# Bringing row 0 of each tile to all partitions: one DMA three units ahead instead of a matmul and a copy

## The chip, the cores and the metric

The kernel runs on one core of a Trainium2 chip. The metric is the device time of one execution in microseconds (us), median of several runs. Nanoseconds are marked ns. The engines are PE (matrix multiply), PEld (its weight loads), DVE (vector), ACT (scalar, activations), POOL (GpSimd) and SP (here it only issues DMAs).

## The reference

```python
def _attn_ref(x):                          # x: (8, 3008, 256) float32
    X = np.fft.fft(x, axis=1)
    X = np.fft.fft(X, axis=2)
    return X.real.astype(np.float32)

def _moe_ref(x, w_gate, w_val, w_out):     # x: (24064, 256), d_ff = 1536
    g = x @ w_gate
    silu = g * (1.0 / (1.0 + np.exp(-g)))
    val = x @ w_val
    return (silu * val @ w_out).astype(np.float32)
```

A two-dimensional Fourier transform mixes the tokens, then a gated feed-forward block follows. The output is float32 of shape (24064, 256).

## The kernel before

The kernel folds the transform's symmetries. It works on 24 tiles of up to 512 columns (a column stands for two output tokens, "plus" and "minus"). `Pt` and `Qt` hold the two halves of a tile's transform, with the feature index d on partitions. A tile has 12 units, one for each 128 of the 1536 hidden features. In each unit PE makes five matmuls of 512 columns (two gate, one value, and in the next unit's time one more of each) and eight output matmuls of 256 columns for the tile before.

For tiles from the fourth on (`split`), the value path also needs row d=0 of `Qt`, times a weight per hidden feature. That row lies in partition 0, and DVE and ACT need it in all 128 partitions. The kernel gets it there with a matmul whose stationary operand `sel` has ones in row 0 and zeros elsewhere, and an ACT copy from PSUM to the tile `bc`:

```python
psG = tile_pool(name="psG", bufs=3, space=PSUM)   # g: gate and broadcast
psV = tile_pool(name="psV", bufs=3, space=PSUM)   # v: value
psO = tile_pool(name="psO", bufs=2, space=PSUM)   # o: output
bcp = tile_pool(name="bc", bufs=2)
# ... (cut)
SEEDED = (3, 5, 7, 9, 11)
def seed(u):                     # v starts from bc * w0, written by ACT
    seeds[u] = psV.tile([P, T], F32, name="v")
    nc.scalar.activation(seeds[u][:, :w], bc[t][:, :w], AF.Copy, scale=w0[:, f:f + 1])

def part_a(u):                                        # ... (cut)
    g = psG.tile([P, T], F32, name="g")
    mm(g, Wp, 0, Pt, True, False)                                    # L743
    mm(g, Wq, 0, Qt, False, True)
    # ... v from the seed, or a new one
    mm(v, Wp, 1, Pt, not ahead, False)
    nc.scalar.activation(sg[:, :w], g[:, :w], AF.Silu)               # L756
    if ahead:
        nc.scalar.copy(es[:, :w], v[:, :w])                          # L759
    else:
        nc.vector.scalar_tensor_tensor(es[:, :w], bc[t][:, :w], w0[:, f:f + 1], v[:, :w],
                                       op0=Alu.mult, op1=Alu.add)    # L761

def part_b(u):                   # one unit later; ... (cut)
    nc.tensor.matmul(g, Wm, Qt, ...)                                 # L779
    nc.tensor.matmul(v, (Wm if seeded(u) else Wq), Qt, ...)          # L782
    # DVE: vm = 2 es - v (L789); ACT: second Silu of g (L791); DVE: hp = sp * v (L797)

for i, u in enumerate(units):
    t, f = u
    if f == 0 and split(u):
        ps = psG.tile([P, T], F32, name="g")
        nc.tensor.matmul(ps[:, :w], sel, pq_tiles(t)[1][:, :w], start=True, stop=True)   # L919
        bc.pop(t - 2, None)
        bc[t] = bcp.tile([P, T], BF16, name="bc")
        nc.scalar.copy(bc[t][:, :w], ps[:, :w])                                          # L922
    # ... (cut)
    run_loads(3)                 # up to three input loads on SP's queue
    part_a(u)
    if owork: owork.run(4)       # output matmuls of the tile before; every 24th step ends a
                                 # pair: ACT copies it, SP stores it
    # ... seed of the next unit, part_b of the unit before, owork.run(4), folds
    if i in job_at: transform(*job_at[i])   # writes Pt or Qt of a later tile
```

All DMAs of the main loop go through SP's queue, in program order. The kernel orders its instructions by hand; semaphores hold back an instruction until what it reads has been written.

## Time and profile before

| | before |
|---|---|
| time, median of 3 runs | 644.68 us |
| PE busy, of a span of 643.8 us | 632.8 us |
| ACT busy | 532.6 us |
| DVE busy | 522.0 us |
| DMA queue of SP, share of 16 engines | 29.5% |
| broadcast matmuls / copies | 21 / 21 |

The page's busy times and the chain of work that ended last (shares of the span by engine, then by line):

```profile
PE 632.8 (98%) x4179; PEld 405.0 (63%) x4179; DVE 522.0 (81%) x945; ACT 532.6 (83%) x975; POOL 452.3 (70%) x419
...
PE 95%; DVE 2%; POOL 1%; ACT 1%; issue 1%; DVEq 0%; ACTq 0%; POOLq 0%
```

PE bounds this kernel. Now the timeline of PE around the broadcast of one tile. The columns are the start, the modelled duration, engine, line, operation, operands and count:

```profile
308.32 0.60 PE L692 MATMUL o<-Wo,hm 128*128 128x256 bf16 x4
308.76 0.38 PE L919 MATMUL g<-Qt,sel 128*128 128x512 bf16 x1
309.18 0.38 PE L743 MATMUL g<-Pt,Wp 128*128 128x512 bf16 x1
309.39 0.38 PE L743 MATMUL g<-Qt,Wq 128*128 128x512 bf16 x1
```

A matmul's end is modelled by the profile: its duration (0.38 us) is longer than the distance between starts (0.21 us), so durations overlap and a "busy" PE need not be streaming. The starts are what to read. From 309.18 to 309.39 is 0.21 us, the pace of a 512-column stream; the Trainium skill (TensorE: Matmul & The Clock Gate, "Wait — 56ns, not 53.3ns?") measured 215.7 ns for it, and this trace agrees. From the broadcast to the next matmul it is 0.42 us, twice that, although PE counts as busy. ACT at the same time:

```profile
308.46 0.67 ACT L791 ACTIVATE sv<-g 128x512 f32<-128x512 f32 x1
309.18 0.59 ACT L922 CAST bc<-g 128x512 bf16<-128x512 f32 x1
```

The gate matmul starts just after ACT's second Silu has let go of a g buffer (308.46 + 0.67 = 309.13). The whole tile, by the windows view (length; busy time and count of PE, PEld, DVE, ACT, POOL; granted clock; DMA share; GB/s):

```profile
308.76:332.73 23.97, 23.93 (x159) 15.34 (x157) 19.79 (x32) 21.53 (x40) 18.84 (x16) 1.00 0.20 58
```

### The profile page before, as it was taken

The page shows a single profiled execution, that of the slowest core. Times are in us where ns is not written, and L with a number is a line of the kernel's source. Part 1 is how long each engine was busy: PE and PEld are TensorE (multiplying, and loading weights), DVE is VectorE, ACT ScalarE, POOL GpSimd, SP SyncE. Part 2 cuts the span into 40 slices and gives each one's busy share as a digit, 9 for nine tenths or more (in the row PEclk, how much of TensorE's full clock was granted, in tenths as well). Part 3 has the DMA queues.
Part 4 walks back from the last instruction along what each step waited for, and adds up shares of the span by engine and source line. Part 5 has one row for each costly group of instructions (what it writes and reads, how often), then busy time and mean ns, then how long its engine had stood idle before and what let it go on. Part 6 is the DMA issues. An engine that isn't in the chain of part 4 may idle for free.

```text
span 643.8 us, 12739 instructions
## 1 busy us (share of the span) xinstructions
PE 632.8 (98%) x4179; PEld 405.0 (63%) x4179; DVE 522.0 (81%) x945; ACT 532.6 (83%) x975; POOL 452.3 (70%) x419
## 2 busy tenths in 40 slices
PE   8999999999999999999999999999999999999997
PEld 5446666666666666666666666666666666666676
DVE  8788667888888888888888888888888888788872
ACT  7586666888888889888888888888898888988983
POOL 8796854798776898896876777877777434444441
PEclk8999999999999999999999999999999999999999
DMA  9746446344314313435135112125111111111112
GB/s 216 134 71 131 117 116 162 97 131 110 100 50 116 99 37 115 127 98 112 50 97 118 49 35 67 52 76 135 50 44 41 43 41 40 43 50 34 50 50 74
DMA packets 46685, 54.35 MB, mean 84 GB/s; under 512 B 6515, under 2 KB 33691, under 8 KB 46619
## 3 DMA queue, kind: packets, MB, share of 16 engines
q1 hardware_dynamic: 43434, 51.19, 29.5%
q0 software_dynamic: 3184, 2.36, 2.8%
q8 instruction: 32, 0.52, 0.4%
q14 instruction: 35, 0.28, 0.2%
HBM read 29.39 MB, written 24.65 MB: 84 GB/s over the span
## 4 chain that ended last, share of the span: by engine, by line
PE 95%; DVE 2%; POOL 1%; ACT 1%; issue 1%; DVEq 0%; ACTq 0%; POOLq 0%
PE o L692 38%; PE g L743 19%; PE v L743 11%; PE g L779 9%; PE v L782 8%; PE g L587 2%; PE o L587 2%; PE v L799 1%; PE v L438 1%; PE g L438 1%; PE g L919 1%; DVE hp L770 1%; PE g L564 1%; PE o L447 0%; PE o L564 0%
## 5 line engine op out<-in xcount | busy, mean ns | idle before, releaser
L794 POOL TENSOR_TENSOR hm<-sv 128x1024 bf16<-128x1024 f32 (+2 forms) x126 | 234.1, 1858 | 154.1 <-ACT sv L791 133.9
L789 DVE SCALAR_TENSOR_TENSOR sv<-es,v 128x512 f32<-128x512 f32 (+2 forms) x252 | 170.8, 678 | 73.5 <-PE v L782 69.8
L756 ACT ACTIVATE sp<-g 128x512 f32<-128x512 f32 (+2 forms) x252 | 149.3, 593 | 48.3 <-PE g L743 46.5
L692 PE MATMUL o<-Wo,hp 128*128 128x256 bf16 (+2 forms) x1140 | 169.7, 273 | 0.0
L692 PE MATMUL o<-Wo,hm 128*128 128x256 bf16 (+2 forms) x1140 | 169.6, 273 | 0.0
L797 DVE TENSOR_TENSOR hp<-sp,v 128x512 bf16<-128x512 f32 (+2 forms) x252 | 168.9, 670 | 0.0
L791 ACT ACTIVATE sv<-g 128x512 f32<-128x512 f32 (+2 forms) x252 | 162.8, 646 | 6.9 <-PE g L779 6.9
L692 PEld LDWEIGHTS <-hm 128*128 128x128 bf16 (+2 forms) x1140 | 111.9, 98 | 72.3 <-issue 5.3
L692 PEld LDWEIGHTS <-hp 128*128 128x128 bf16 (+2 forms) x1140 | 112.1, 99 | 69.4
L761 DVE SCALAR_TENSOR_TENSOR es<-bc,w,v 128x512 f32<-128x512 bf16 (+2 forms) x147 | 107.5, 731 | 4.2 <-PE v L743 4.2
L743 PE MATMUL g<-Pt,Wp 128*128 128x512 bf16 (+2 forms) x288 | 107.9, 375 | 0.8
L743 PE MATMUL g<-Qt,Wq 128*128 128x512 bf16 (+2 forms) x288 | 107.9, 375 | 0.5 <-DVE Qt L600 0.5
L743 PE MATMUL v<-Pt,Wp 128*128 128x512 bf16 (+2 forms) x288 | 107.8, 374 | 0.1
L779 PE MATMUL g<-Qt,Wm 128*128 128x512 bf16 (+2 forms) x288 | 107.9, 375 | 0.0
L743 PEld LDWEIGHTS <-Wp 128*128 128x128 bf16 x576 | 56.3, 98 | 40.0 <-issue 2.5
L732 ACT ACTIVATE v<-bc,w 128x512 f32<-128x512 bf16 (+2 forms) x105 | 73.2, 697 | 0.5 <-DVE hp L797 0.5
L698 ACT COPY ev<-o 128x512 f32<-128x512 f32 x90 | 53.5, 595 | 8.4 <-PE o L692 5.8
L759 ACT COPY es<-v 128x512 f32<-128x512 f32 (+2 forms) x105 | 60.3, 574 | 0.0
L782 PE MATMUL v<-Qt,Wq 128*128 128x512 bf16 (+2 forms) x147 | 55.1, 375 | 0.0
L743 PEld LDWEIGHTS <-Wq 128*128 128x128 bf16 x324 | 31.6, 98 | 15.7 <-issue 6.6
L157 POOL TENSOR_TENSOR SDf<-XA 128x1020 f32<-128x1020 f32 x14 | 33.0, 2355 | 11.3 <-DMA St<-Fc 6.6
L782 PE MATMUL v<-Qt,Wm 128*128 128x512 bf16 (+2 forms) x105 | 39.4, 375 | 0.0
(175 smaller groups left out, 629.6 us busy)
## 6 DMA issues: line engine op xcount, KB each, us to landing
out_dram<-ev SPq DMA_DIRECT2D x96, 128.0 KB
XA<-in_x_dram SPq DMA_DIRECT2D x32, 256.0 KB
XA<-in_x_dram SPq DMA_DIRECT2D x112, 64.0 KB
XC<-in_x_dram SPq DMA_DIRECT2D x32, 120.0 KB
XC<-in_x_dram SPq DMA_DIRECT2D x105, 32.0 KB
St<-Fc SPq DMA_DIRECT2D x14, 128.5 KB
out_dram<-ev SPq DMA_DIRECT2D x12, 120.0 KB
out_dram<-ev SPq DMA_DIRECT2D x10, 112.0 KB
```

Source lines behind the costliest of these rows:

```text
L692: nc.tensor.matmul(ps[:n, j, :], hts[minus][:, f, c:c + n], Wo[:, f, :], start=(f == 0), stop=(f == nF - 1))
L732: nc.scalar.activation(seeds[u][:, :w], bc[t][:, :w], AF.Copy, scale=w0[:, f:f + 1])
L743: nc.tensor.matmul(ps[:, :w], Wt[:, gv, fs], src[:, :w], start=start, stop=stop, skip_group_check=True)
L756: nc.scalar.activation(sg[:, :w], g[:, :w], AF.Silu)
L759: nc.scalar.copy(es[:, :w], v[:, :w])
L761: nc.vector.scalar_tensor_tensor(es[:, :w], bc[t][:, :w], w0[:, f:f + 1], v[:, :w], op0=Alu.mult, op1=Alu.add)
L779: nc.tensor.matmul(g[:, :w], Wm[:, 0, fs], Qt[:, :w], start=False, stop=True, skip_group_check=True)
L782: nc.tensor.matmul(v[:, :wp], (Wm if seeded(u) else Wq)[:, 1, fs], Qt[:, :wp], start=False, stop=True, skip_group_check=True)
L789: nc.vector.scalar_tensor_tensor(vm[:, w - 1::-1], es[:, :w], 2.0, v[:, :w], op0=Alu.mult, op1=Alu.subtract)
L791: nc.scalar.activation(sm[:, w - 1::-1], g[:, :w], AF.Silu)
L794: nc.gpsimd.tensor_tensor(hts[t][1][:, f - n + 1:f + 1, :w], sv[:, 0:n, :w, 1], sv[:, 0:n, :w, 0], op=Alu.mult)
L797: nc.vector.tensor_tensor(hts[t][0][:, f, :wp], sp[:, :wp], v[:, :wp], op=Alu.mult)
```

## The change

It should take the broadcast off PE and ACT: a DMA, which uses neither, copies row 0 of the next tile's `Qt` to 128 partitions, issued three units before that tile. The fourth tile keeps the matmul, because its row is written only at unit 10 of the tile before.

```diff
-        if f == 0 and split(u):
+        if f == 0 and split(u) and t not in bc:
             ps = psG.tile([P, T], F32, name="g")
             w = width(t) + (B if t == nT - 1 else 0)
             nc.tensor.matmul(ps[:, :w], sel, pq_tiles(t)[1][:, :w], start=True, stop=True)
-            bc.pop(t - 2, None)
             bc[t] = bcp.tile([P, T], BF16, name="bc")
             nc.scalar.copy(bc[t][:, :w], ps[:, :w])
+        if f == 9 and split(u) and t + 1 < nT:
+            w = width(t + 1) + (B if t + 1 == nT - 1 else 0)
+            bc[t + 1] = bcp.tile([P, T], BF16, name="bc")
+            nc.sync.dma_start(out=bc[t + 1][:, :w], in_=pq_tiles(t + 1)[1][0:1, :w].unsqueeze(1).to_broadcast([1, P, w]))
```

## The prediction

> **What bounds the kernel.** The tensor engine. The chain of work that ended last is 95% PE; the page has PE busy for 632.8 of 643.8 us at full clock. The start times in the PE timeline show it closer: from 105 us on one matmul follows the other at the streaming pace (512 columns every 0.216 us), and a unit of a tile takes 1.95 us. ACT (83%) and DVE (81%) keep up; ACT is the closer (21.5 of 24.0 us in a tile without transform work, by the windows view).
>
> **What the change removes.** 20 of 21 broadcast matmuls (line 919) and of 21 ACT copies (line 922, 0.586 us each, 11.7 us of ACT). The matmul alone would be worth 0.216 us, but in the timeline the broadcast starts at 308.76 and the next matmul at 309.18. I read: the broadcast takes one of three g buffers in PSUM, so the gate matmul behind it needs the buffer that ACT's second Silu of two units before (308.46 to 309.13) still reads. Over tiles 5 to 24 the distance to the next matmul is 0.41 to 0.42 us (once 0.37): 8.25 us in sum, half matmul, half buffer wait. All of it is PE time on the critical path; without the broadcast the gate matmul finds a buffer long free.
>
> **What it adds.** 20 DMAs of 128 KB (128 rows of 1 KB, all read from one partition) on SP's queue. By the order of instructions, DVE waits for their landing at a tile's first es, where it waited for ACT. The nearest thing in the trace, the fold spread (128.5 KB, SBUF to SBUF), lands 2.3 to 2.8 us after its issue. The new one reads a single partition: the Trainium skill (SBUF — State Buffer, Door 1: the DMA port swizzle) gives 27.2 GB/s a port, so I estimate 4.8 us for 131 KB, about 7 us to landing if one port limits it; no run here shows that yet. Three units of program order are 5.9 us, too little for that, but SP runs ahead of it: before, it waits from 300.0 to 305.2 for the output copy that comes just after the new DMA, with the next tile at 308.8. So the DMA should go out some 9 us ahead of its tile and land 2 us or more in time; less where input loads are queued.
>
> **What stays.** The wait of 0.13 us per tile for the seed at unit 7, where ACT is late. The rest of ACT's gain hides under PE.
>
> **Time.** 644.68 - 8.25 = 636.4 us, 1.3% less; range 635.4 to 638.6. Faster by over 2%: 0.02; within 2%: 0.93; slower by over 2%: 0.05.
>
> **What the profile would show.** Line 919 once; a tile without transform 23.55 us instead of 23.97; ACT busy 521 us; es at line 761 waiting for PE's v as before, not for a DMA; no new idle time on PE.
>
> **What would make it wrong.** The DMA landing later than its tile's first es: then es, the value buffer's release and PE stall by the difference, up to 20 times. Input loads, or DVE's Q row, ahead of the DMA in SP's queue would do the same. Every eighth DMA waits for an earlier one's landing, so a slow one also holds back stores and loads, but those have slack.

## The result, and the profile after

The changed kernel takes 638.08 us (637.58 to 638.66, 4 runs), the kernel before 644.7 us (4 runs). The ratio is 0.9899, with a 95% interval of 0.9881 to 0.9916. All ratios here are the mean time of one kernel's fast runs over that of the other's of the same rounds, so not quite the ratio of the medians. The output is correct. This is 6.6 us or 1.0% less; 636.4 us were forecast, and the range (635.4 to 638.6) held it, near its upper end. The forecast gain of 8.25 us would be a ratio of 0.9872, outside the interval, so something is missing.

The same parts of the page after; the last line is the group of es on DVE (busy, mean ns of one, idle time before it and what ended it):

```profile
PE 624.6 (98%) x4159; PEld 402.1 (63%) x4159; DVE 518.7 (82%) x945; ACT 520.8 (82%) x955; POOL 452.8 (71%) x419
...
PE 90%; DMA 6%; DVE 2%; SPq 1%; ACT 1%; issue 0%; DVEq 0%; ACTq 0%
...
L761 DVE SCALAR_TENSOR_TENSOR es<-bc,w,v 128x512 f32<-128x512 bf16 (+2 forms) x147 | 107.2, 729 | 3.4 <-DMA bc<-Qt 3.2
```

PE has 20 matmuls and 8.2 us of busy time less, ACT 11.8 us. But DMA now stands in the chain with 6%: the new DMA is 2% of it, and the rest are input loads, mostly at the kernel's start, which the chain reaches by way of SP's queue. And es, which in the kernel before waited only for PE's v (4.2 us), waits 3.2 us for the new DMA. The share of SP's DMA queue rises from 29.5% to 39.3%. PE at the start of the same tile, and that tile in the windows view:

```profile
306.33 0.60 PE L692 MATMUL o<-Wo,hm 128*128 128x256 bf16 x4
306.76 0.38 PE L743 MATMUL g<-Pt,Wp 128*128 128x512 bf16 x1
306.98 0.38 PE L743 MATMUL g<-Qt,Wq 128*128 128x512 bf16 x1
```

```profile
306.76:330.32 23.56, 23.56 (x158) 15.27 (x156) 19.64 (x32) 20.96 (x39) 18.50 (x16) 1.00 0.34 64
```

The gate matmul follows the output matmuls at their pace, and the tile is 0.41 us shorter, as predicted. So most tiles gave what was expected. Where are the other 1.6 us? The waits view has only two waits of es for the DMA (total us, times, longest):

```profile
DVE es L761 <- DMA bc<-Qt: 3.2, 2, 2.0
```

They belong to the 5th and the 10th tile. The 5th in full: first what SP issued, then DVE, then PE. In brackets stands the idle time before an instruction and what ended it.

```profile
119.48 0.84 SPq L704 DMA_DIRECT2D out_dram<-ev  x2
120.37 3.72 SPq L142 DMA_DIRECT2D XC<-in_x_dram  x4
124.14 0.64 SPq L144 DMA_DIRECT2D XC<-in_x_dram  x1
124.82 0.47 SPq L140 DMA_DIRECT2D XC<-in_x_dram  x1
125.39 0.58 SPq L925 DMA_DIRECT2D bc<-Qt  x1
```

```profile
132.10 0.75 DVE L761 SCALAR_TENSOR_TENSOR es<-bc,w,v 128x512 f32<-128x512 bf16 x1 [1.96 <-DMA bc<-Qt]
```

```profile
132.10 0.38 PE L779 MATMUL g<-Qt,Wm 128*128 128x512 bf16 x1
132.90 0.38 PE L782 MATMUL v<-Qt,Wq 128*128 128x512 bf16 x1 [0.42 <-DVE es L761]
133.12 0.49 PE L692 MATMUL o<-Wo,hp 128*128 128x256 bf16 x3
134.03 0.28 PE L692 MATMUL o<-Wo,hp 128*128 128x256 bf16 x1 [0.43 <-DVE hp L797]
```

SP spent 4.8 us issuing six input loads, then issued the broadcast at 125.39, only 3.7 us before the tile's first gate matmul at 129.09. It landed 6.6 us later (from the trace's semaphore updates). es started about 2 us late, and PE lost about 0.6 us at L782 (0.80 between starts instead of 0.22) and 0.6 at the next hp. Compare a quiet tile, the one shown above that starts at 306.76:

```profile
298.00 0.52 SPq L925 DMA_DIRECT2D bc<-Qt  x1
303.19 1.18 SPq L704 DMA_DIRECT2D out_dram<-ev  x3
```

Here the DMA goes out 8.8 us ahead of the tile: SP has nothing left to issue before it, and after it stands waiting for the next output copy until 303.19. It landed at 304.4, over 3 us before it was needed. Of the 20 DMAs, 12 landed more than 2 us before their tile's first es started, six 0.1 to 2 us before it, and two were late.

### The profile page after: what moved, and what is told of

Same layout as the page of the kernel before. It is cut to its first block, busy times and chain, and to the rows that moved or that the text cites. A ratio compares the mean times of both kernels' runs of the same rounds, so it can differ in the third digit from the quotient of the medians.

```text
span 635.8 us, 12736 instructions
## 1 busy us (share of the span) xinstructions
PE 624.6 (98%) x4159; PEld 402.1 (63%) x4159; DVE 518.7 (82%) x945; ACT 520.8 (82%) x955; POOL 452.8 (71%) x419
## 3 DMA queue, kind: packets, MB, share of 16 engines
q1 hardware_dynamic: 46314, 53.77, 39.3%
## 4 chain that ended last, share of the span: by engine, by line
PE 90%; DMA 6%; DVE 2%; SPq 1%; ACT 1%; issue 0%; DVEq 0%; ACTq 0%
PE o L692 38%; PE g L743 18%; PE v L743 10%; PE g L779 9%; PE v L782 8%; DMA XC<-in_x_dram 3%; PE g L587 2%; DMA bc<-Qt 2%; PE o L587 2%; PE v L799 1%; DMA XA<-in_x_dram 1%; SPq L142 1%; DVE hp L770 1%; PE g L564 0%; PE o L564 0%
## 5 line engine op out<-in xcount | busy, mean ns | idle before, releaser
L782 PE MATMUL v<-Qt,Wq 128*128 128x512 bf16 (+2 forms) x147 | 55.1, 375 | 0.4 <-DVE es L761 0.4
L782 PE MATMUL v<-Qt,Wm 128*128 128x512 bf16 (+2 forms) x105 | 39.3, 375 | 0.0
```

Of the source, the lines that this page charges most:

```text
L782: nc.tensor.matmul(v[:, :wp], (Wm if seeded(u) else Wq)[:, 1, fs], Qt[:, :wp], start=False, stop=True, skip_group_check=True)
```

## The experiments

Theory: the gain is PE time, 0.216 us of matmul and 0.2 us of waiting for a PSUM buffer in each of 20 tiles, and two late tiles give 1.6 us back. Rivals: the gain comes from relieving ACT; the loss is spread over all tiles by DMA traffic; the second half of the broadcast's 0.42 us is a fixed cost of loading other weights. Experiments ran; each was compared with runs of the kernel before on the same chip.

### e1_early: the DMA at unit 6 instead of unit 9

```diff
-        if f == 9 and split(u) and t + 1 < nT:
+        if f == 6 and split(u) and t + 1 < nT:
```

Unit 6 is the earliest place: `transform` writes the next tile's `Qt` up to unit 5, and a DMA that stands before that write in the program would read old data.

> The broadcast DMA is placed at unit 6 instead of unit 9, the first unit after the last write of the next tile's Q row; nothing else moves. Theory: the 1.6 us that the change missed (638.1 instead of 636.5) are two tiles alone, the 5th and the 10th, whose DMA was issued only 3.7 and 4.5 us before its tile behind input loads in SP's queue and landed 2.1 and 1.4 us after the value matmul's end. Then this run takes 636.3 to 636.8 us and no es waits for a DMA. Rival: the loss is spread over all tiles (more DMA traffic, other engines slowed): then 637.8 to 638.4 us.

Measured: 636.41 us (635.58 to 637.14, 4 runs), ratio to before 0.9870 (0.9856 to 0.9883), correct. What ended idle time ahead of the instructions that use bc:

```profile
its engine sat idle before it (us, times) until:
  DVE hp L797: 0.5, 2
  PE g L919: 0.3, 1
  PE v L743: 0.2, 1
```

No instruction waits for the DMA any more. The two tiles in the windows view, in the changed kernel:

```profile
129.09:153.92 24.83, 23.97 (x158) 15.47 (x156) 19.44 (x32) 20.95 (x40) 22.49 (x20) 1.00 0.58 112
254.76:280.86 26.10, 25.72 (x171) 16.33 (x168) 21.71 (x38) 21.92 (x41) 23.02 (x20) 1.00 0.58 122
```

And in e1_early:

```profile
128.96:152.54 23.58, 23.56 (x159) 15.56 (x156) 19.54 (x32) 21.03 (x40) 22.45 (x20) 1.00 0.55 116
253.38:278.86 25.48, 25.48 (x171) 16.43 (x169) 21.77 (x38) 21.92 (x41) 22.98 (x20) 1.00 0.54 116
```

They are 1.25 and 0.62 us shorter, together 1.9 us; the medians differ by 1.7. The load on the DMA queues in these windows is nearly the same (0.54 to 0.58), and e1_early still issues all 20 DMAs, so the rival of spread DMA cost falls. With the DMA in time, the time is what the prediction's sum said.

### e2_dead_matmul and e3_dead_matmul_64: the matmul put back without its copy

```diff
+        elif f == 0 and split(u):
+            ps = psG.tile([P, T], F32, name="g")
+            w = width(t) + (B if t == nT - 1 else 0)      # e3: w = 64
+            nc.tensor.matmul(ps[:, :w], sel, pq_tiles(t)[1][:, :w], start=True, stop=True)
         if f == 9 and split(u) and t + 1 < nT:
```

> The changed kernel with the broadcast matmul put back where it was, 512 columns into a g buffer that nobody reads; no ACT copy. Theory: the gain was PE time, 0.216 us of matmul and 0.2 us of waiting for a g buffer in each of 20 tiles, so all of it goes: 645 to 646.5 us, and the next matmul starts 0.41 us after the dead one. Rival: the gain came from relieving ACT of 20 copies: then it stays near 638 to 640 us.

> As e2_dead_matmul, but the dead matmul streams 64 columns instead of 512 (0.03 us instead of 0.216). Theory: the following gate matmul waits for the g buffer until ACT's second Silu of two units before has ended, an instant that does not depend on the dead matmul; so the distance from dead matmul to gate matmul stays 0.39 to 0.42 us and the time is that of e2_dead_matmul within 0.5 us (645 to 646.5). Rival 1: a fixed cost of 0.2 us for the extra weights: distance 0.23 us, 642 to 643 us. Rival 2: the matmul's own stream alone: 638.5 to 639 us.

Measured: 645.74 us for e2 and 645.62 us for e3 (5 runs each); both ratios to before are 1.0011 (0.9998 to 1.0023). Both are correct. PE in e2:

```profile
309.63 0.38 PE L925 MATMUL g<-Qt,sel 128*128 128x512 bf16 x1
310.05 0.38 PE L743 MATMUL g<-Pt,Wp 128*128 128x512 bf16 x1
```

PE in e3:

```profile
309.69 0.19 PE L925 MATMUL g<-Qt,sel 128*128 128x64 bf16 x1
310.10 0.38 PE L743 MATMUL g<-Pt,Wp 128*128 128x512 bf16 x1 [0.22 <-ACT sv L791]
```

The matmul alone takes the whole gain away, so it was PE time and not ACT's relief. (e2 lies 1.0 us above the kernel before; its 5th tile still waits 2.0 us for a late DMA.) And an eighth of the matmul costs just as much: the next gate matmul starts 0.41 us after it either way. With the short one the idle time is no longer hidden under the modelled duration, and the trace names what ended it, in all 20 tiles: ACT's second Silu, which frees the g buffer. A fixed cost of the weights would have given 642 to 643 us. Making the broadcast matmul narrower gains nothing as long as the pool has three g buffers: the stream runs inside the wait for the buffer. What a fourth g buffer would give was not tried.

### e4_dead_copy: the ACT copy put back without its matmul

```diff
+        elif f == 0 and split(u):
+            w = width(t) + (B if t == nT - 1 else 0)
+            nc.scalar.copy(sgp.tile([P, T], F32, name="sg")[:, :w], Wp[:, 0, :w])
         if f == 9 and split(u) and t + 1 < nT:
```

> The changed kernel with an ACT copy of 128x512 put back at the same place (constant data into an unused buffer), no matmul. Theory: ACT's 0.59 us per tile hide under PE: 637.8 to 638.6 us, ACT busy 11 us more than in the changed kernel. Rival: ACT's relief was a part of the gain: 640 us or more (if all of it, up to 649).

Measured: 638.07 us (637.42 to 638.32, 4 runs), ratio 0.9894 (0.9879 to 0.9909), against 638.08 us of the changed kernel. ACT's 20 copies cost nothing. One number was missed: ACT's busy time rose by 6.3 us (520.8 to 527.1), not 11. The copies are in the trace with a median of 622 ns each; in busy time, stretches in which instructions overlap count once.

### e5_own_row and e8_sixteen_rows: what makes the DMA slow (wrong results on purpose)

```diff
-in_=pq_tiles(t + 1)[1][0:1, :w].unsqueeze(1).to_broadcast([1, P, w])
+in_=pq_tiles(t + 1)[1][:, :w]                                            # e5
+in_=pq_tiles(t + 1)[1][0:16, :w].unsqueeze(1).to_broadcast([16, 8, w])   # e8
```

> Wrong result on purpose: the DMA of the changed kernel, same place, same 128 rows of 1 KB to the same tile, but each partition receives its own row of Qt instead of row 0. Theory: the 6.3 to 6.6 us to landing come from reading one partition, and the two late tiles from that: landing falls to 2.0 to 3.0 us (as the fold spread of like size), no es waits for it, time 636.2 to 637.0. Rival: 128 rows of 1 KB within SBUF take 6 us whatever the source: landing and time as in the changed kernel (638.1).

> Wrong result on purpose: as e5_own_row, but the source is rows 0 to 15, each to 8 partitions. If the limit is the port that the skill's table gives to several partitions (rows 0 to 15 lie on 4 ports[...]): landing about 1 us above that of e5_own_row. If the limit is the single partition (16 of them): landing within 0.3 us of e5_own_row.

Both gave the wrong output (relative error 0.12). From issue to landing, by the semaphore updates, in tiles with quiet queues: 6.3 us in the changed kernel, 3.1 us with 16 source rows, 2.0 us with each partition's own row. The bytes and the destinations are the same in all three. Time of e5: 635.86 us (635.76 to 636.81, 4 runs), ratio 0.9863 (0.9849 to 0.9876), a little below the expected 636.2 to 637.0, and no instruction waits for the DMA, although it stands at unit 9. e8: one look, 636.68 us (a single run, its state unknown).

So the time comes from the source. The Trainium skill (SBUF — State Buffer, Door 1: the DMA port swizzle) puts rows 0 to 15 on 4 ports of four of these rows each. A quarter of the excess of one partition (6.3 - 2.0 = 4.3) is 1.1 us, and e8 shows 1.1 us; a sixteenth would be 0.3. That is what a limit of the port, not of the single partition, gives. It is one point, and a partition-wise limit with some other share is not excluded. Another rival, that one DMA engine does the whole broadcast alone, falls by the trace's DMA packet records in the quiet tile at 298.00: from 1.2 to 5.9 us after the issue some 16 packets of 1 KB are under way at once, most of them taking about 0.5 us. That is 131 KB in about 4.7 us, or 28 GB/s; in e8 the same bytes take about 1.4 us.

### e6_late: the DMA at unit 10

```diff
-        if f == 9 and split(u) and t + 1 < nT:
+        if f == 10 and split(u) and t + 1 < nT:
```

> The changed kernel with the DMA at unit 10 instead of unit 9, which puts it behind the third pair of output stores in SP's order, for which SP waits until some 2.4 us before the tile. Theory: it lands 6.5 us after its issue, so 3.3 us after the end of the tile's first value matmul; in the changed kernel PE lost that lateness less 0.8 us in the two late tiles, so here 2.5 us in each of 20 tiles: 675 to 692 us. Rival: lateness is absorbed and the two tiles suffered from the input loads: then 638 to 642 us.

Measured: 709.47 us (698.97 to 710.73, 4 runs), ratio of the fast runs 1.0916 (1.0842 to 1.0991), correct. Two of the four runs, the profiled one among them, are slow, so small differences are not read from it; an effect of 9% is far beyond that. The waits view, three of its lines (the last two are PE's loss, first at L782, then at the next hp, where its weight load waits):

```profile
DVE es L761 <- DMA bc<-Qt: 67.2, 20, 4.7
...
PE v L782 <- DVE es L761: 37.6, 20, 3.2
...
PEld L692 <- DVE hp L797: 15.2, 20, 0.8
```

es waits for the DMA in all 20 tiles, and PE loses 52.8 us, 2.6 per tile, in line with the 2.5 expected. Lateness is not absorbed, whatever else is in the queue. But the time is above the range expected. The windows view of one tile shows why (third column from the right: the granted clock of PE):

```profile
303.88:308.75 4.87, 2.23 (x14) 1.18 (x13) 2.12 (x4) 1.69 (x3) 1.43 (x2) 1.00 0.61 126
308.97:312.36 3.39, 3.39 (x13) 1.80 (x12) 2.72 (x6) 1.92 (x3) 2.25 (x3) 0.50 0.55 137
312.36:314.33 1.97, 1.97 (x14) 1.29 (x13) 0.84 (x3) 1.26 (x3) 1.74 (x1) 0.99 0.85 126
```

After the idle time of PE its clock is halved for 3.4 us. The trace's clock records have 13 such stretches before the last matmul, so 13 times 3.41 times one half, 22 us. 636.4 + 53 + 22 = 711; the profiled run took 710.7. The expectation had left the clock out. The fast runs show the same: the mean granted clock was 0.968 and 0.971 in the two slow runs, 0.985 and 0.971 in the two fast ones, and the core's span times its clock is 686 to 688 us in all four. So what tells these runs apart is how often the clock was halved.

### e7_early_four_seeds and e10_before_four_seeds: the wait that the prediction said would stay

```diff
-    SEEDED = (3, 5, 7, 9, 11)
-    SEEDED_END = (3, 5, 7, 9, 11)
+    SEEDED = (2, 5, 8, 11)
+    SEEDED_END = (2, 5, 8, 11)
```

e7 is e1_early with this edit, e10 the kernel before with it.

> e1_early with the seeded units 2, 5, 8, 11 instead of 3, 5, 7, 9, 11, so that no seed follows an output copy on ACT (those fall in units 0, 3, 6, 9). The prediction said that a wait of 0.13 us per tile for the seed at unit 7 stays because ACT is late there. If so, it goes: 633.4 to 634.4 us (636.4 less 21 times 0.13). Rival: the wait has another cause, or the extra es moved to DVE takes its place: 636 us or more.

> The kernel before, with only the seeded units changed to 2, 5, 8, 11, to tell whether the gain of e7_early_four_seeds over e1_early (2.4 us) needs the broadcast DMA. Theory: the 0.13 us per tile at unit 7 goes here too, 641.5 to 642.5 us. Rival: with the broadcast copy still on ACT at unit 0, the seed for unit 2 comes late and a wait at unit 2 takes the place: 643 to 645 us.

PE at unit 7 in the kernel before, where v is late by 0.13 us (0.35 between starts):

```profile
322.84 0.38 PE L743 MATMUL g<-Pt,Wp 128*128 128x512 bf16 x1
323.06 0.38 PE L743 MATMUL g<-Qt,Wq 128*128 128x512 bf16 x1
323.41 0.38 PE L743 MATMUL v<-Pt,Wp 128*128 128x512 bf16 x1
```

ACT just before it: the seed, which writes v, starts behind the output copy and ends at 323.36.

```profile
322.18 0.59 ACT L698 COPY ev<-o 128x512 f32<-128x512 f32 x1
322.66 0.70 ACT L732 ACTIVATE v<-bc,w 128x512 f32<-128x512 bf16 x1
```

The same place in e7:

```profile
318.09 0.38 PE L743 MATMUL g<-Qt,Wq 128*128 128x512 bf16 x1
318.30 0.38 PE L743 MATMUL v<-Pt,Wp 128*128 128x512 bf16 x1
```

Measured: e7 633.97 us (632.74 to 634.73, 5 runs), ratio 0.9830 (0.9814 to 0.9846); e10 642.11 us (641.73 to 642.9, 5 runs), ratio 0.9953 (0.9939 to 0.9966). Both are correct. The seed of unit 7 had followed an output copy on ACT; moving the seeds away from those copies gains 2.4 to 2.7 us with or without the DMA. The edit also makes four seeds of five, so part of the gain could come from the lighter ACT; no run keeps five seeds and only moves them. The size, 21 times 0.13 us or 2.7 us, is that of the wait alone. The two gains add up, and e7 beats both kernels: 0.9830 of the time before, where the changed kernel has 0.9899.

## Why the prediction was right or wrong

- **PE bounds the kernel; 8.25 us in sum: right. "Half matmul, half buffer wait": right as a count, but not two separate costs.** e2 puts the matmul back and lands at the time before. e3 shows that the buffer sets the sum: with an eighth of the stream the wait fills its place. With the DMA in time (e1) the kernel takes 636.41 us, the predicted 636.4. That it agrees to 0.1 us is luck: the runs of e1 spread from 635.58 to 637.14, and e5, also with no late tile, took 635.86.
- **ACT's gain hides under PE: right.** e4 puts the copy back at no cost. ACT busy was predicted at 521 us and is 520.8.
- **About 7 us to landing if one port limits it: right, a little high.** 6.3 us in quiet tiles; e5 and e8 show that the source makes it.
- **"So the DMA should go out some 9 us ahead of its tile and land 2 us or more in time; less where input loads are queued": right for 12 of 20 tiles, short of it in six without loss, wrong in two.** This is the step that fell short, by the missing 1.6 us. The prediction saw the queued loads but costed nothing for them in its sum; its range was wide enough to hold them. SP needed 3.72 us merely to issue four loads of 60 rows, and the lead of the 5th and 10th tile shrank to 3.7 and 4.5 us.
- **"es at line 761 waiting for PE's v as before, not for a DMA; no new idle time on PE": wrong in those two tiles,** right in the others. The prediction had listed just this among the things that would make it wrong.
- **The unit-7 wait stays: right** (e1 and the changed kernel still have it), and its cause, a late ACT, agrees with the trace and with e7.

"Within 2%" held, with 0.93 on it.

## What to carry to other kernels

When a matmul looks cheap, measure the distance between starts, not its duration: here a matmul of 0.216 us cost 0.41 us because it took a PSUM buffer out of a pool of three, and shrinking it to an eighth gained nothing. A DMA that replaces compute must be placed by when its queue will reach it, not by where it stands in the program; check the lead tile by tile, because a few tiles with queued loads set the loss. A late operand can cost PE twice, once by waiting and once by a slower clock afterwards.

## What the Trainium skill lacked or had wrong

- SBUF — State Buffer (Door 1: the DMA port swizzle): it has the port table and 27.2 GB/s a port, but does not say that a broadcast from one partition is held to that. Measured: 128 KB land 6.3 us after issue from one partition, 3.1 from 16, 2.0 from 128. The last tile's 84.0 KB (in thousands of bytes) instead of 131.1 landed after 4.65 instead of 6.34 us in the changed kernel, so 47.1 KB in 1.69 us or 28 GB/s; in e1_early 4.58 instead of 6.59 us, 23 GB/s. The page's figure lies between, and near the 28 GB/s of the packet records.
- TensorE: Matmul & The Clock Gate (Part 1: The HAM clock gate; HAM oscillation): the abstract rule there is no PE idle gap above about 3.4 us, though the page also tells of a kernel whose short idle times made the clock swing, without their length. In e6_late the clock was halved for 3.413 us around idle gaps of 1.5 to 3.2 us by the modelled ends (most with a second gap of 0.5 us behind them), 13 times in 20 tiles; others of 1.8 to 1.95 us had no such effect. So in this case a gap under 3.4 us was not safe.
- TensorE: Matmul & The Clock Gate: it says that the number of slow matmuls at a kernel's start varies from run to run with the phase of the clock's window, and of the size only that it is under 1% of a typical kernel's span. Measured: the profiled run of before had a half-clock stretch of 3.4 us at 12.8 us and made its first broadcast at 105.2 us; that of the changed kernel had none and made it at 104.2, although the two do the same work up to there. Of all eleven profiled runs, the six with such a stretch made it at 105.1 to 105.3 us, the five without at 104.0 to 104.6. A difference of 1 us between two profiles need not be the change.
- None of the pages read gives the time that SP itself takes to issue a DMA by its shape: four loads of 60 rows took 3.72 us of SP's time (median in the changed kernel 0.88 us each), while loads of 128 rows took 0.60 us each and loads of 4 rows 0.3 us (medians).
